# One call of a weight load moved ahead in a fused attention and GLU kernel: the first raw weights of f follow the first operands of q and M in the load queue

## The chip, the core and the metric

The kernel runs on one core of one Trainium2 chip. Its metric is the device time of one execution in microseconds (us), lower being better. Before the change it takes 731.56 us, the median of three runs (731.47 to 731.98).

## What is computed

All tensors are float32; S = 2048 tokens, D = 640, 32 heads of 20, F = 1536. The inputs are x, the weights wqkv, wo, w_gate, w_up, w_down, and a vector gate_w.

```python
qkv = (x @ wqkv).reshape(B, S, 3, H, Dh)            # q, k, v per head
phi = lambda t: where(t > 0, t + 1, exp(t)) + 1e-6
pq, pk = phi(q), phi(k)
kv  = einsum("bhsd,bhse->bhde", pk, v);  z = einsum("bhsd->bhd", pk)
num = einsum("bhqd,bhde->bhqe", pq, kv); den = einsum("bhqd,bhd->bhq", pq, z)
a = (num / (den + 1e-6)) @ wo                        # linear attention block
b = (sigmoid(x @ w_gate) * (x @ w_up)) @ w_down      # gated linear unit
g = sigmoid((x * gate_w).sum(-1))
out = g * a + (1 - g) * b
```

## The kernel before

**Numbers.** Every large float32 product is made of three matmuls: each operand is split into a high part (rounded to the matmul's format, written by ScalarE, ACT) and a low part (the rest, by a subtraction on VectorE, DVE), and TensorE (PE) adds high by high, low by high and high by low (helper `mm3`, lines 407 to 409; the split is lines 420 and 424). A split therefore is one ACT instruction and one DVE instruction, in that order.

**Stages.** The tokens are four groups of 512 columns, worked on in two pairs; pair 1 here is the first. The stages, in order of time, are: the k products and G = x^T phi(k); then, in `q_phase`, the q products of the first pair of groups, with the attention matrices M made beside them; then, in `f_phase`, the GLU of that pair; then q and GLU of the other pair with the weight forms read back from scratch memory; at the end the products with M and the output. The products of a pair use a seven-product scheme for two by two blocks: a unit n such as ("q", 1, 0) or ("f", 1, 0) goes through steps s1 to s7 (class `Block`), and needs three forms of its weights, wg (form 0), wu (form 1) and ws (form 2, sums of blocks, made in two parts).

**Weights of a unit.** `load_w` (line 1300) takes the next unit of the list `w_loads`, which is q(1,0), f(1,0), f(1,1) and so on, and issues one DMA of 640 KB from SyncE's queue (SP) into the next of the two buffers of the tile `wst`. The two buffers are used in turn. `queue_g` and `queue_s` then queue the work that makes the forms out of it: the split to wg, the split to wu, five sums on DVE that are made in place, and two splits to ws (`s_part`, line 1353: part 0 of 640 columns, part 1 of 512 columns). Behind the low part of part 1, the last reader of the buffer, `s_part` calls `load_w` (line 1362) for the next unit. Two more calls stand by themselves: line 1560, before M's first loads, for q(1,0), and line 2273 in `q_phase`, at step s6 of its unit A, for f(1,1).

**The order of work around the change.** In `q_phase` of pair 1 PE works through A = q(1,2), whose forms come ready from scratch memory, and B = q(1,0), whose forms are made from `wst`: A1, A2, two plain units, B1, B2, A3 to A7, B3 to B7. Between these stand the pieces of M for six groups of heads: `kv_part` (line 1624; a product on PE into PSUM tile `rot`, line 1629, then kvt, kvh, kvl on DVE) and `m_part` (line 1640; six matmuls of 320 columns with woh, wol, kvh, kvl into two PSUM tiles, each copied out to `ms`). The wo weights of a group come by a DMA into `wo_sb` (two buffers) and are split to woh and wol by `wo_split` (line 1612), which also issues the load of the group after next. `kv_part(5)` and `m_part(2)` stand between A5 and A6, `m_part(3)` between A7 and B3, `m_part(4)` and `m_part(5)` between B4, B5 and B6.

**Who orders it.** PE's order is written out by hand in the code. ACT's and DVE's is made while the program is built: a planner (class `Order`) keeps an estimated time of every engine and of every DMA, and each time that PE's work has been added, it adds those pieces of queued work whose data would have come and which would not delay PE (`fill`, line 116). A piece that is urgent (`first=True`: the split to wg of f(1,0), the wo splits) goes ahead of the others as soon as its data is there by that estimate; `order.need(key)` forces a piece out where PE needs it. On the chip each engine runs its list strictly in order, so an instruction that waits holds all behind it. SP's queue is also a list in order: an issue that waits for a buffer holds the issues behind it. GpSimd (POOL) has a queue of its own for the stores: each unit's forms go to scratch memory (wq, wf), each q result to p_dram, each piece of M to m_dram.

The queue of SP at this place: wst of q(1,0) (line 1560), three wv_sb, two wo_sb, then ws and wu of q(1,2) (lines 1662 and 1663), and from there only loads that other work calls for as buffers come free.

Of the kernel before, what the change touches and what calls it, by code (L numbers as in the profile page):

```python
# [367 lines left out]
def a_cost(w):  # L368
    return 0.06 + w / 1200

def v_cost(w):
    return 0.07 + w / 960

@with_exitstack
def gated_mix_kernel(ctx: ExitStack, tc: tile.TileContext, xt, xn, wk, wv, wo, wst_q, wst_f, out_t):
# [6 lines left out]
    order = Order()  # L382
# [3 lines left out]
    def f32(ap):  # L386
        return ap.bitcast(F32)
# [49 lines left out]
    def split(hi, lo, src, after=""):  # L437
        act(hi, src, AF.Copy, after)
        at = order.act + A_LAG

        def low():
            order.vec = max(order.vec, at)
            vec2(lo, src, f32(hi), OP.subtract)
        order.then(low)

    def add(out, a, b, after=""):
        vec2(out, a, b, OP.add, after)

    def sub(out, a, b, after=""):
        vec2(out, a, b, OP.subtract, after)  # L450
# [680 lines left out]
    for c in range(1, 4):  # L1131
# [37 lines left out]
        if c == 3:  # L1169
# [19 lines left out]
            def put(n, i, t):  # L1189
                WT[n, i] = t  # L1190
                W[n, i] = [t[:, c] for c in range(2)]

            def store_w(n, i):

                key = n[::2] + (i,)
                w_dram[key] = dram.tile(list(WT[n, i].shape), F32, name="w%s%d%d" % key)
                gp.dma_start(w_dram[key], f32(WT[n, i]))
# [81 lines left out]
    def wu_tile():  # L1279
        return pw.tile([P, 2, 3 * P], F32R, name="wu", tag="wu", bufs=2)  # L1280
# [3 lines left out]
    def ws_tile():  # L1284
        ws_n.append(0)
        return (pz if len(ws_n) % 2 == 0 else pw).tile([P, 2, 9 * P], F32R, name="ws", tag="ws")

    def load_form(n, i):
        t = (wg_tile, wu_tile, ws_tile)[i]()
        w = t.shape[2]  # L1290
        for c0, c1 in ((0, 2 * P), (7 * P, w), (5 * P, 7 * P), (2 * P, 5 * P)) if n == ("f", 0, 0) and i == 2 else ((0, w),):
            sp.dma_start(f32(t[:, :, c0:c1]), w_dram[n[::2] + (i,)][:, :, c0:c1])
        put(n, i, t)
# [6 lines left out]
    def load_w():  # L1300
        t = pw2.tile([P, 2, D], F32, name="wst", tag="wst", bufs=2)
        if not w_loads:
            t = t.rearrange("p k c -> p (k c)").rearrange("p (k c) -> p k c", c=CW)
            sp.dma_start(t, xt[len(c1_x), :, :, CW:])
            c1_x.append(t)
            other[-1].at = order.when(t)
            return
        n = w_loads.pop(0)
        sp.dma_start(t, wst_f[n[2], :, 0:2] if n[0] == "f" else wst_q[:, 0:2])
        WST[n] = t  # L1310
        W_AT[n] = t
# [10 lines left out]
    def w_due(n, s):  # L1322
        return {"stream": ("w", n), "due": order.due((*n[1:], s))} if n[0] == "f" and n[1:] + (1,) in order.plan else {}
# [6 lines left out]
    def queue_s(n, first=0, last=2):  # L1330

        def sums(part):
            g, u = WST[n][:, 0], WST[n][:, 1]
            c = [slice(2 * i * P, 2 * (i + 1) * P) for i in range(2)]
            if part == 0:
                order.need(("wg", n), False)
                order.need(("u", n), False)
                add(u[:, c[1]], u[:, c[0]], u[:, c[1]])
                sub(u[:, c[0]], g[:, c[0]], u[:, c[0]])
            else:  # L1340
                sub(g[:, c[0]], u[:, c[1]], g[:, c[0]])
                sub(g[:, c[1]], g[:, c[1]], g[:, c[0]])
                sub(g[:, 4 * P:], g[:, 4 * P:], u[:, 4 * P:])
            SUM_AT[n, 1 - part] = order.vec + V_LAG

        def u_part():
            put(n, 1, wu_tile())
            split(*W[n, 1], WST[n][:, 1, 2 * P:])
            order.then(lambda: store_w(n, 1))

        cut = (0, 5 * P, 9 * P)

        def s_part(part):
            if part == 0:
                put(n, 2, ws_tile())
            h, l = W[n, 2]
            cs = slice(cut[part], cut[part + 1])
            order.act = max(order.act, SUM_AT[n, part])
            split(h[:, cs], l[:, cs], WST[n][:, part, :cut[part + 1] - cut[part]])
            if part:  # L1360
                order.then(lambda: store_w(n, 2))
                order.then(load_w)

        if first == 0:
            order.add(a_cost(3 * P), v_cost(3 * P), u_part, ("u", n), lambda: order.when(W_AT[n]) if n in W_AT else 1e9, **w_due(n, 3))
            order.add(0, 2 * v_cost(2 * P), lambda: sums(0), **w_due(n, 3))
            order.add(0, 3 * v_cost(2 * P), lambda: sums(1), **w_due(n, 3))
        if last > 1:
            for part in range(2):
                w = cut[part + 1] - cut[part]  # L1370
                order.add(a_cost(w), v_cost(w), lambda part=part: s_part(part), ("w", n, part),
                          lambda part=part: SUM_AT.get((n, part), 1e9), **w_due(n, 3 + part))
# [288 lines left out]
    sp.t = max(sp.t, freed[1])  # L1661
    load_form(("q", 1, 2), 2)
    load_form(("q", 1, 2), 1)

    down_pool, down_cms = [], []
    HT, DST, WD, DS, DS_AT = {}, {}, {}, {}, {}
# [1395 lines left out]
```

## Time and profile before

| what | value |
|---|---|
| time, median of three runs | 731.56 us |
| the profiled execution, its own time | 731.82 us |
| span of the profile, first to last instruction | 730.1 us |
| TensorE busy (matmuls) | 719.4 us, 99% of the span |
| VectorE busy | 583.3 us, 80% |
| ScalarE busy | 371.0 us, 51% |
| GpSimd busy | 117.1 us, 16% |
| mean granted TensorE clock | 0.995 of full speed |
| DMA | 191.95 MB, mean 263 GB/s |

How to read it: the page gives one execution. Its time stands 1.7 us above its span, for what lies before the first and behind the last instruction, and 0.26 us above the median of the runs. A timeline row gives the start of an instruction, its length, engine, line and tiles (out<-in), and in brackets the idle time of the engine just before it with what ended that. Rows of PE overlap, since a matmul's end is modelled: a matmul of 512 columns has a length of 0.39 us, but the next starts 0.23 us after it. SPq and POOL rows of DMA are issues, not transfers.

### The profile page before, as it was taken

How to read it: one execution, taken by the hardware profiler on the slowest of the kernel's cores; microseconds unless marked ns; L12 is line 12 of the kernel's file. 1: busy time of each engine (PE TensorE's matmuls, PEld its weight loads, DVE VectorE, ACT ScalarE, POOL GpSimd, SP SyncE). 2: the span in 40 equal slices, each digit the busy share in tenths (PEclk: the TensorE clock that was granted, in tenths of full speed). 3: DMA queues.
4: the chain of work that ended last, by engine and by line, in shares of the span. 5: the costliest groups of instructions: out<-in, count | busy, mean ns of one | idle time of the engine just before them, and what ended most of it. 6: DMA issues, size and time to landing. Idle time of an engine off the chain costs nothing.

```text
span 730.1 us, 9886 instructions
## 1 busy us (share of the span) xinstructions
PE 719.4 (99%) x3395; PEld 607.4 (83%) x3395; DVE 583.3 (80%) x1009; ACT 371.0 (51%) x685; POOL 117.1 (16%) x189
## 2 busy tenths in 40 slices
PE   9999999996999999999999999999999999999998
PEld 8999898885888888888888888888888888888887
DVE  6888878784778889898989988357696968799895
ACT  6784647363755763535354855345424241544451
POOL 0211113132311221311211134001010111002300
PEclk9999999998999999999999999999999999999999
DMA  7677687967867866767787979978979895959957
GB/s 255 160 224 184 181 203 185 346 198 276 290 235 263 317 228 244 260 225 267 273 293 291 311 254 346 410 260 269 357 251 309 258 391 180 408 214 336 225 104 236
DMA packets 78889, 191.95 MB, mean 263 GB/s; under 512 B 8394, under 2 KB 37018, under 8 KB 75126
## 3 DMA queue, kind: packets, MB, share of 16 engines
q1 hardware_dynamic: 57654, 117.72, 48.9%
q0 software_dynamic: 20896, 73.36, 30.1%
q8 instruction: 27, 0.44, 0.2%
q10 hardware_dynamic: 288, 0.23, 0.1%
q14 instruction: 24, 0.20, 0.1%
HBM read 113.46 MB, written 75.52 MB: 259 GB/s over the span
## 4 chain that ended last, share of the span: by engine, by line
PE 93%; DMA 3%; DVE 2%; ACT 1%; SPq 0%; issue 0%; ACTq 0%; DVEq 0%
PE ch L407 11%; PE ch L408 11%; PE ch L409 11%; PE cc L407 9%; PE cc L408 9%; PE cc L409 9%; PE dd L407 6%; PE dd L408 6%; PE dd L409 6%; PE rot L407 5%; PE rot L409 5%; PE rot L408 5%; DMA ws<-wq 1%; DMA wst<-wst_f 1%; PE dd L2787 1%; DVE xtl L424 1%
## 5 line engine op out<-in xcount | busy, mean ns | idle before, releaser
L420 ACT ACTIVATE c<-ch 128x512 f32<-128x512 f32 x54 | 32.2, 596 | 81.2 <-PE ch L409 80.3
L424 DVE TENSOR_TENSOR hf<-c,hf 128x512 fp32r<-128x512 f32 x80 | 54.4, 686 | 19.3 <-ACT hf L420 18.9
L420 ACT ACTIVATE hf<-c 128x512 fp32r<-128x512 f32 x80 | 49.0, 625 | 31.1 <-DVE c L424 31.0
L424 DVE TENSOR_TENSOR c<-cc,c 128x512 f32<-128x512 f32 x42 | 28.9, 688 | 27.4 <-PE cc L409 17.9
L408 PE MATMUL ch<-xtl,ws 128*128 128x512 f32 x112 | 43.6, 389 | 0.0
L407 PE MATMUL ch<-xth,ws 128*128 128x512 f32 x112 | 43.6, 389 | 0.0
L409 PE MATMUL ch<-xth,ws 128*128 128x512 f32 x112 | 43.6, 389 | 0.0
L424 DVE TENSOR_TENSOR c<-c,c 128x512 f32<-128x512 f32 x52 | 35.7, 687 | 3.3 <-ACT c L420 2.7
L424 DVE TENSOR_TENSOR tb<-rot,tb 128x512 f32<-128x512 f32 x56 | 36.1, 682 | 0.3 <-PE rot L409 0.3
L407 PE MATMUL dd<-xrh,wg 128*128 128x512 f32 x90 | 35.1, 390 | 0.0
L408 PE MATMUL dd<-xrl,wg 128*128 128x512 f32 x90 | 35.0, 389 | 0.0
L409 PE MATMUL dd<-xrh,wg 128*128 128x512 f32 x90 | 35.0, 389 | 0.0
L420 ACT ACTIVATE c<-dd 128x512 f32<-128x512 f32 x22 | 13.1, 596 | 41.4 <-PE dd L409 41.3
L407 PE MATMUL cc<-xbh,ws 128*128 128x512 f32 x84 | 32.9, 392 | 0.0
L408 PE MATMUL cc<-xbl,ws 128*128 128x512 f32 x84 | 32.9, 392 | 0.0
L409 PE MATMUL cc<-xbh,ws 128*128 128x512 f32 x84 | 32.9, 392 | 0.0
L424 DVE TENSOR_TENSOR tb<-dd,tb 128x512 f32<-128x512 f32 x36 | 24.7, 686 | 9.3 <-PE dd L409 9.2
L420 ACT ACTIVATE dd<-ch 128x512 f32<-128x512 f32 x22 | 12.8, 582 | 35.9 <-PE ch L409 35.9
L407 PE MATMUL ch<-xth,wu 128*128 128x512 f32 x56 | 22.5, 402 | 6.1 <-ACT c L420 6.1
L424 DVE TENSOR_TENSOR tb<-cc,tb 128x512 f32<-128x512 f32 x36 | 24.5, 684 | 1.9 <-PE cc L409 1.9
L424 DVE TENSOR_TENSOR wst<-wst 128x256 f32<-128x256 f32 (+1 forms) x65 | 24.6, 395 | 1.4
L409 PEld LDWEIGHTS ch<-xth,ws 128*128 128x128 f32 x112 | 21.0, 188 | 4.7 <-DVE ws L424 0.2
(690 smaller groups left out, 2329.2 us busy)
## 6 DMA issues: line engine op xcount, KB each, us to landing
wf<-ws POOLq DMA_DIRECT2D x12, 1152.0 KB, 7.5
ws<-wf SPq DMA_DIRECT2D x11, 1152.0 KB, 8.1
wst<-wst_f SPq DMA_DIRECT2D x12, 640.0 KB, 4.9
wf<-wg POOLq DMA_DIRECT2D x12, 640.0 KB, 6.5
wd<-wd POOLq DMA_DIRECT2D x12, 640.0 KB, 7.7
wg<-wf SPq DMA_DIRECT2D x12, 640.0 KB, 5.3
wf<-wd SPq DMA_DIRECT2D x10, 640.0 KB, 11.6
xnst<-xn SPq DMA_DIRECT2D x16, 320.0 KB, 4.0
```

The source lines that it names most:

```text
L407: nc.tensor.matmul(out, l_hi, r_hi, start=first, stop=False, skip_group_check=True)
L408: nc.tensor.matmul(out, l_hi, r_lo, start=False, stop=False, skip_group_check=True)
L409: nc.tensor.matmul(out, l_lo, r_hi, start=False, stop=last, skip_group_check=True)
L420: nc.scalar.activation(out, src, fn, **kw)
L424: nc.vector.tensor_tensor(out, a, b, op=op)
L2787: nc.tensor.matmul(ps, l, r, start=new, stop=j == 1 and k == ks[-1], skip_group_check=True)
```

## The change

The call of `load_w` behind the last split of a unit's raw weights is made only for units of f. A call for f(1,0) is added right behind the two loads of q(1,2)'s forms ws and wu, at the head of the stage. The list of loads is the same, with the same two buffers, and so is the call at step s6 of A for f(1,1).

```diff
             split(h[:, cs], l[:, cs], WST[n][:, part, :cut[part + 1] - cut[part]])
             if part:
                 order.then(lambda: store_w(n, 2))
-                order.then(load_w)
+                if n[0] == "f":
+                    order.then(load_w)
...
     load_form(("q", 1, 2), 2)
     load_form(("q", 1, 2), 1)
+    load_w()
```

On SP's queue, at the head of the q stage, the order shows one load in another place; wst<-wst_f is the load of an f unit's raw weights, ws<-wq and wu<-wq are the forms of q(1,2).

```order
 L364 DMA ws<-wq_470 128x2304
 L364 DMA wu<-wq_469 128x768
+L364 DMA wst<-wst_f 128x1280
 L364 DMA wo_sb<-wo 100x640
 L364 DMA wv_sb<-wv 128x500 x2
 L364 DMA wo_sb<-wo 100x640
 L364 DMA wv_sb<-wv 128x500
-L364 DMA wo_sb<-wo 100x640
-L364 DMA wst<-wst_f 128x1280
-L364 DMA wo_sb<-wo 100x640
+L364 DMA wo_sb<-wo 100x640 x2
 L364 DMA wst<-wst_f 128x1280 x2
```

The load of f(1,0) has moved ahead of six loads of M's operands; the loads of wo for groups 4 and 5 now stand together.

On ACT, between steps A3 and A6, the planner places the splits otherwise; c_1624 and c_1803 are results of q, dd and ms belong to `m_part`, wg<-wst is the split of f(1,0), ws<-wst the last split of q(1,0). Before:

```order
L420 ACTIVATE c_1624<-c_1624 128x512
L420 ACTIVATE ms<-dd_1816 120x320
L420 ACTIVATE ms<-dd_1821 120x320
L420 ACTIVATE woh<-wo_sb 100x640
L420 ACTIVATE ws<-wst 128x512
L420 ACTIVATE woh<-wo_sb 100x640
L420 ACTIVATE wg<-wst 128x640
L420 ACTIVATE c_1883<-ch_1616 128x512
L420 ACTIVATE ms<-dd_1896 100x320
L420 ACTIVATE ms<-dd_1901 100x320
L420 ACTIVATE woh<-wo_sb 100x640
L420 ACTIVATE qe<-c_1883 128x512
```

And after the change (c_1626 is the tile that was c_1624):

```order
L420 ACTIVATE c_1626<-c_1626 128x512
L420 ACTIVATE wg<-wst 128x640
L420 ACTIVATE ms<-dd_1818 120x320
L420 ACTIVATE ms<-dd_1825 120x320
L420 ACTIVATE woh<-wo_sb 100x640 x2
L420 ACTIVATE ws<-wst 128x512
L420 ACTIVATE c_1883<-ch_1618 128x512
L420 ACTIVATE ms<-dd_1896 100x320
L420 ACTIVATE ms<-dd_1901 100x320
L420 ACTIVATE qe<-c_1883 128x512
L420 ACTIVATE c_1883<-c_1883 128x512
L420 ACTIVATE woh<-wo_sb 100x640
```

The split to wg of f(1,0) no longer stands right ahead of c_1883<-ch, the copy that empties the PSUM tile of A5, but five instructions further up; the split to woh of group 4 stands two rows later.

On DVE at the same place the low parts follow; kvt, kvh, kvl belong to `kv_part` of groups 3 and 4, the first wol<-wo_sb to group 2. Before:

```order
L428 SCALAR_TENSOR_TENSOR qe<-qe,c_1624 128x512
L424 TENSOR_TENSOR kvt<-rot_1827,bd 100x100
L868 CAST kvh<-kvt 100x100
L424 TENSOR_TENSOR kvl<-kvt,kvh 100x100
L424 TENSOR_TENSOR wol<-wo_sb,woh 100x640
L424 TENSOR_TENSOR kvt<-rot_1841,bd 100x100
```

And after:

```order
L428 SCALAR_TENSOR_TENSOR qe<-qe,c_1626 128x512
L424 TENSOR_TENSOR wg<-wst,wg 128x640
L424 TENSOR_TENSOR kvt<-rot_1831,bd 100x100
L868 CAST kvh<-kvt 100x100
L424 TENSOR_TENSOR kvl<-kvt,kvh 100x100
L424 TENSOR_TENSOR kvt<-rot_1848,bd 100x100
L868 CAST kvh<-kvt 100x100
L424 TENSOR_TENSOR kvl<-kvt,kvh 100x100
L424 TENSOR_TENSOR wol<-wo_sb,woh 100x640 x2
```

The low part of group 2's wo now stands behind wg and behind the kv pieces of both groups 3 and 4. PE's own list is the same before and after. Three smaller moves go with it: on POOL the store of f(1,0)'s wg stands ahead of that of q(1,0)'s ws; and in the first step of `f_phase` the split to wg of f(1,1) stands three rows earlier on ACT (ahead of the load of the sigmoid's table) and two earlier on DVE, with its store one place earlier on POOL.

## Prediction

> **What bounds the kernel now.** First the page: the span, and TensorE's granted clock in 40 slices of 18.25 us.
>
> ```profile
> span 730.1 us, 9886 instructions
> ...
> PEclk9999999998999999999999999999999999999999
> ```
>
> PE is busy for 99% of the span, so its own work is the bound; one slice, the tenth (164 to 182 us), has a lower clock. The waits of PE and then the chain of waits between 155 and 180 us say what happens there.
>
> ```profile
> PE ch L407 <- ACT c L420: 6.1, 1, 6.1
> ```
>
> ```profile
> 164.44 7.22 DMA wst<-wst_f
> ```
>
> One wait of 6.1 us is nearly all that PE loses to other engines. It ends on ACT's copy of a PSUM tile, but the chain runs through that copy back to a load: wst<-wst_f, the raw weights of f(1,0), issued at 164.44 and landed 7.22 us later. The timelines show why a load for a later stage stops PE. SP, the loads:
>
> ```profile
> 135.19 0.42 SPq L364 DMA_DIRECT2D wu<-wq  x1
> 145.60 0.31 SPq L364 DMA_DIRECT2D wo_sb<-wo  x1
> ...
> 164.08 0.30 SPq L364 DMA_DIRECT2D wo_sb<-wo  x1
> ```
>
> ACT, ahead of the stop and at it:
>
> ```profile
> 161.24 0.63 ACT L420 ACTIVATE c<-c 128x512 f32<-128x512 f32 x1
> 161.78 0.75 ACT L420 ACTIVATE ms<-dd 120x320 f32<-120x320 f32 x2
> 162.41 0.74 ACT L420 ACTIVATE woh<-wo_sb 100x640 fp32r<-100x640 f32 x1
> ...
> 171.68 0.74 ACT L420 ACTIVATE wg<-wst 128x640 fp32r<-128x640 f32 x1 [7.37 <-DMA wst<-wst_f]
> 172.32 0.58 ACT L420 ACTIVATE c<-ch 128x512 f32<-128x512 f32 x1
> ```
>
> And PE at the same place:
>
> ```profile
> 164.92 0.31 PE L407 MATMUL dd<-woh,kvh 100*100 100x320 f32 x1
> 165.06 0.30 PE L408 MATMUL dd<-wol,kvh 100*100 100x320 f32 x1
> ...
> 172.95 0.79 PE L407 MATMUL ch<-xth,wu 128*128 128x512 f32 x1 [6.11 <-ACT c L420]
> ```
>
> ACT comes to the split to wg at 164.3 us and sits there for 7.37 us. Right behind it in ACT's list stands c<-ch, which empties the PSUM tile that A5 filled; A6, at 172.95, writes that tile again. A5's matmuls had all started before 164.92, so the copy itself was ready when ACT stopped, within a microsecond.
>
> **The change part by part: what it removes.** The load leaves SP some 29 us sooner, behind wu at 135.19. Even at the 7.22 us of the old load it lands near 143, and at twice that before 151; ACT now comes to wg when it ends c<-c, at 161.87. So the 6.1 us go. A little more goes with them, because that idle time counts from a modelled end: PE's rows overlap by some 0.2 us (164.92 plus 0.31, against the next start at 165.06). I put the hole at 6.3 us. Nothing else is late in its place: the copy then waits only for A5 and ends before 166, and A6 has a `m_part` and a `kv_part` of PE ahead of it until about 166.6.
>
> The hole has a tail. By windows, with the granted clock in the third column from the end: the hole's middle, its end, A6 with A7, and B6 with B7, which are the same eighteen matmuls.
>
> ```profile
> 167.00:171.00 4.00, 0.00 (x0) 0.00 (x0) 0.00 (x0) 0.00 (x0) 0.00 (x0) 1.00 1.02 376
> 171.00:172.95 1.95, 0.00 (x0) 0.00 (x1) 0.51 (x1) 1.27 (x3) 0.00 (x0) 0.61 0.58 244
> 172.95:179.64 6.69, 6.69 (x19) 5.24 (x19) 4.33 (x9) 3.98 (x8) 1.98 (x4) 0.60 0.76 242
> 187.10:191.27 4.17, 4.17 (x21) 3.46 (x19) 2.53 (x5) 2.88 (x6) 1.76 (x4) 1.00 0.77 218
> ```
>
> The clock falls while PE idles and is low for most of A6 and A7: 6.69 us against 4.17. Without the hole it does not fall, so 6.69 - 4.17 = 2.5 us go too. Together 8.8 us.
>
> The Trainium skill, "TensorE: Matmul & The Clock Gate", section "What's actually happening", states that about 3.4 us without work halve the clock and about 3.4 us of work restore it. By that the tail would be half of 3.4, an estimate of 1.7 us, and the time 0.8 us above the one forecast here. The trace agrees on the cause, but its rows show a longer tail, and the measurement decides.
>
> **What it moves.** On DVE, wg and both kv pieces now stand ahead of the wol of group 2, which PE's second matmul of `m_part(2)` reads (the one at 165.06). Before, one kv piece did.
>
> ```profile
> 162.52 0.25 DVE L424 TENSOR_TENSOR kvt<-rot,bd 100x100 f32<-100x100 f32 x1
> ...
> 163.23 0.82 DVE L424 TENSOR_TENSOR wol<-wo_sb,woh 100x640 fp32r<-100x640 f32 x1
> ...
> 172.44 0.83 DVE L424 TENSOR_TENSOR wg<-wst,wg 128x640 fp32r<-128x640 f32 x1 [7.07 <-ACT wg L420]
> 173.19 0.82 DVE L424 TENSOR_TENSOR wol<-wo_sb,woh 100x640 fp32r<-100x640 f32 x1
> ```
>
> wg takes 0.75 us of DVE (172.44 to 173.19), a kv piece 0.71 (162.52 to 163.23). So wol starts at 163.23 + 0.75 + 0.71 = 164.69 and ends, with its 0.82, at 165.51. Its woh is ready: on ACT wg takes 0.64 (171.68 to 172.32), woh moves from 162.41 to 163.05 and ends by 163.8. PE wants wol at 165.06 and waits 0.45, call it 0.5 us: a new stall. Its bounds are nothing, if pieces fit into gaps, and 1.5 us, the whole of the 1.46 put ahead.
>
> In f's first step, the split of f(1,1) now stands ahead of the sigmoid and of the copy behind it, first ACT, then PE:
>
> ```profile
> 196.23 0.60 ACT L420 ACTIVATE c<-ch 128x512 f32<-128x512 f32 x1
> ```
>
> ```profile
> 198.07 0.39 PE L407 MATMUL ch<-xth,ws 128*128 128x512 f32 x1
> ```
>
> The copy ended at 196.83, 1.24 us before PE wanted its tile. Put ahead of it are ACT's wg, 0.64, and, through the sum that the sigmoid reads, DVE's wg, 0.75: 1.39 in all. So 0 to 0.15 us; I take 0.1. The two swaps on POOL are stores to scratch memory that only the other pair's stage reads back; they cost nothing while the DMAs keep up.
>
> The issue itself costs SP 0.4 us, as wu's, where its next issue is at 145.60, ten us later. The load brings 640 KB, 1.7 us at the 376 GB/s of the window 167 to 171, in among the transfers of 136 to 147 us. What is most exposed to it is the chain gt_dram, back, gt; the instructions on the tile back, and its landing times:
>
> ```profile
> L364 POOL DMA_DIRECT2D back<-gt_dram x4: 558/560/581, 145.5 to 147.1; - x4
> L420 ACT ACTIVATE gt<-back x1: 727/727/727, 159.5 to 159.5; 128x640 f32<-128x640 f32 x1
> ...
> DMA to landing us min/median/max: 4.6/5.6/6.0
> ```
>
> The last issue at 147.1 lands by 153.1 with the longest of these, and ACT reads back at 159.5: 6.4 us of cover for 1.7. The wo_sb issued at 145.60 has until 162.41. So the load costs nothing where it goes.
>
> **The sum.** 6.3 + 2.5 - 0.5 - 0.1 = 8.2 us. The profiled execution took 731.82, 1.7 above its span; it would take 723.6, and the median, 0.26 lower, 723.4. All behind this place only moves earlier, since PE waits for nothing there. I add 0.1 for losses that the next rival brings close: 723.5. The forecast's own bounds are 722.7 (no new stall at all: 731.56 - 8.8) and 724.6 (wol's full 1.5 us and 0.15 in f).
>
> **The rivals.** First, a shorter wait takes the old one's place, on ACT at the split of group 4's wo. Its load goes out when group 2's wol has been read: at 164.08 before, right behind 163.23 + 0.82; now at about 165.5. On ACT that split stands ahead of A6's copies, of f(1,0)'s splits and of B5's copy, for which B6 waits. That copy had 0.2 us to spare before, and loads of wv and wo had these landing times (the last column):
>
> ```profile
> 186.41 0.60 ACT L420 ACTIVATE c<-ch 128x512 f32<-128x512 f32 x1 [0.20 <-PE ch L409]
> ```
>
> ```profile
> wv_sb<-wv SPq DMA_DIRECT2D x4, 250.0 KB, 5.1
> ...
> wo_sb<-wo SPq DMA_DIRECT2D x2, 300.0 KB, 7.0
> ```
>
> The copy is due at 186.41 - 8.3 = 178.1. From the split to it ACT has three rows of 640 columns (0.64 each, as 171.68 to 172.32), nine of up to 512 (0.54, as 161.24 to 161.78) and a pair of ms (0.63, as 161.78 to 162.41), an estimate of 7.4 us. So the split must start by 170.7, 5.2 us behind the issue. The row of 5.1 just holds, the row of 7.0 is 1.8 us too long: 725.3. For the forecast: the stretch was full at 376 GB/s with the 640 KB in it, which are now gone from there. For the rival: the store of f(1,0)'s wg now goes ahead. Chance 0.11.
>
> Second, only the wait goes and the clock still falls near here, from several small stalls or by itself: 723.5 + 2.5 = 726.0. Against it, the clock is 1.00 up to 171 us, with 4 us of idleness in that, and falls only then. Chance 0.05.
>
> Third, the change does not do what it says: ACT's copy was held by something that ended together with the load, and the wait stays: 731.6. Against it, nothing stands between wg and the copy in ACT's list, and DVE's 7.07 us end on the same split. Chance 0.03.
>
> Fourth, slower: the early load holds up the transfers beside it. "DMA: Bandwidth & Descriptors" of the Trainium skill, section "Issuing engines are not separate DMA queues", states that transfers run on the same 16 engines and interleave, whichever engine issued them. The mechanism here is ACT's gt<-back: if back lands late, ACT's list stops, and with it A3's copy and PE. It begins to cost at 6.4 us of delay, one for one, and makes the kernel slower from 6.4 + 8.1 = 14.5; at 16 us the time is 723.5 + 9.6 = 733.1. For it, the two wo loads issued shortly ahead took 7.0 us for 300 KB (the row above), so transfers crowd here already; against it, 1.7 us of added transfer would have to grow ninefold. No run shows such a delay. Chance 0.03.
>
> **How the numbers follow.** The forecast has 0.78, the rivals 0.11, 0.05, 0.03 and 0.03. A difference under 0.2% (1.5 us) could not be told from none here. The forecast and the first two rivals are faster by more than that: 0.94; the third is the same, 0.03; the fourth slower, 0.03. The range runs from the forecast's lower bound, 722.7, to the second rival, 726.0. The predicted time is the forecast's, 723.5.
>
> **What would show it.** In the profile after, the 6.1 us wait is gone from PE's waits, the tenth slice has a full clock, and A6 with A7 take 4.2 us. The load is issued near 136, and ACT's wg runs at 162 with no idle time ahead. A wait of PE of 0.5 us on DVE's wol near 165 would confirm the new stall. ACT idle at the woh of group 4, and PE at B6, would be the first rival; a half clock without a hole the second; the old 7.4 us at something else the third; idle time ahead of gt<-back the fourth. The prediction is wrong if PE's time from 164.92 to the end of A7, 14.7 us before, does not fall to about 6.4, or if as much is lost again behind it.

## The result and the profile after

The changed kernel takes 726.55 us, the median of four runs (726.34 to 727.22), against 731.51 for the kernel before in runs beside it: a ratio of 0.9932, 95% interval 0.9915 to 0.9949. Measured again (run e5 below) it takes 726.29, ratio 0.9923 (0.9909 to 0.9936). So it is faster by about 5 us, and 3 us slower than forecast: outside the range. The profiled execution took 726.68 us.

The hole is gone, and its tail with it. The page, PE's waits, and the window of A6 and A7:

```profile
span 725.0 us, 9883 instructions
...
PEclk9999999999999999999999999999999999999999
```

```profile
PE dd L407 <- DVE c L424: 0.6, 1, 0.6
PE cc L407 <- DVE c L424: 0.5, 1, 0.5
PE dd L408 <- DVE wol L424: 0.5, 1, 0.5
PE dd L407 <- DVE ms L868: 0.3, 1, 0.3
```

```profile
168.19:172.36 4.17, 4.17 (x21) 3.45 (x20) 1.69 (x5) 1.57 (x3) 1.60 (x3) 1.00 0.92 249
```

The wait of 6.1 us no longer stands among PE's waits, the tenth slice has a full clock, and A6 with A7 take 4.17 us and not 6.69. Four small waits are listed instead; the first, 0.6 us on DVE's c, lies at 160.05, ahead of the hole's place, and was 0.3 us before the change. PE's list is the same in both kernels, so the start of each matmul can be compared one by one; where the distance between the two traces jumps, PE gained or lost time, and below this is called the loss "by the starts":

| place in the trace after | change, us | forecast |
|---|---|---|
| hole and half clock, to the end of A7 | -8.83 | -8.8 |
| `m_part(2)`, 166.6, on wol | +0.69 | +0.5 |
| `m_part(5)` and B7, 179.4 and 183.1, on DVE's ms and c | +1.22 | 0 |
| first step of f, 188.8 (0.33) and 192.6 (0.39) | +0.73 | +0.1 |
| first 7 us of the kernel (0.61), and 160.0 (0.30) | +0.90 | 0 |
| everywhere else | +0.14 | 0 |
| sum | -5.15 | -8.2 |

Two engines show how the third row comes about. SP and ACT after the change:

```profile
138.20 0.33 SPq L364 DMA_DIRECT2D wst<-wst_f  x1
...
166.54 1.21 SPq L364 DMA_DIRECT2D wo_sb<-wo  x2
```

```profile
162.69 0.72 ACT L420 ACTIVATE wg<-wst 128x640 fp32r<-128x640 f32 x1
...
169.15 0.63 ACT L420 ACTIVATE c<-c 128x512 f32<-128x512 f32 x1
172.05 0.74 ACT L420 ACTIVATE woh<-wo_sb 100x640 fp32r<-100x640 f32 x1 [2.28 <-DMA wo_sb<-wo]
```

The early load is issued at 138.2 (near 136 was forecast), and wg is split at 162.69 with no idle time. But the loads of wo for groups 4 and 5 wait for a buffer until 166.54, and ACT comes to group 4's split 3.2 us later and idles for 2.28 us. Before, ACT came to it 9.4 us after the issue (164.08), because it had stood in the hole. The row of before:

```profile
173.43 0.75 ACT L420 ACTIVATE woh<-wo_sb 100x640 fp32r<-100x640 f32 x1
```

DVE and PE behind it, after the change:

```profile
172.82 0.83 DVE L424 TENSOR_TENSOR wol<-wo_sb,woh 100x640 fp32r<-100x640 f32 x1 [2.32 <-ACT woh L420]
...
175.01 0.55 DVE L424 TENSOR_TENSOR wu<-wst,wu 128x384 fp32r<-128x384 f32 x1
...
178.85 0.88 DVE L868 COPY ms<-dd 100x320 f32<-100x320 f32 x2
...
182.32 0.68 DVE L424 TENSOR_TENSOR c<-cc,c 128x512 f32<-128x512 f32 x1
```

```profile
179.39 0.39 PE L407 MATMUL dd<-woh,kvh 100*100 100x320 f32 x1 [0.27 <-DVE ms L868]
...
183.06 0.50 PE L407 MATMUL cc<-xbh,ws 128*128 128x512 f32 x1 [0.47 <-DVE c L424]
```

From wu on DVE has no gap down to c, and PE waits for two of its results. In the first step of f the chain of waits runs back to a store:

```profile
181.36 5.51 DMA p_dram<-qe
...
186.95 0.64 ACT qe L420
...
188.73 0.63 ACT wg L420
...
190.82 0.61 DVE c L424
...
191.45 1.13 ACT c L420 x2
...
192.62 0.50 PE ch L407
```

The group of tiles that qe belongs to has four buffers, and the new qe at 186.95 takes the one whose store to p_dram went out at 181.36 and landed 5.5 us later. The split of f(1,1), wg at 188.73, stands in the same chain. So two things delay PE in this step, the store and that split; e2 and e7 below tell them apart.

### The profile page after: what moved, and what is told of

Same layout as the page of the kernel before. It is cut to its first block, busy times and chain, and to the rows that moved or that the text cites. A ratio compares the mean times of both kernels' runs of the same rounds, so it can differ in the third digit from the quotient of the medians.

```text
span 725.0 us, 9883 instructions
## 1 busy us (share of the span) xinstructions
PE 718.9 (99%) x3395; PEld 606.2 (84%) x3395; DVE 583.1 (80%) x1009; ACT 371.1 (51%) x685; POOL 116.8 (16%) x189
## 4 chain that ended last, share of the span: by engine, by line
PE 91%; DMA 3%; issue 2%; DVE 2%; POOL 1%; ACT 1%; POOLq 0%; ACTq 0%; DVEq 0%
PE ch L407 10%; PE ch L408 10%; PE ch L409 10%; PE cc L407 8%; PE cc L408 8%; PE cc L409 8%; PE dd L407 6%; PE dd L408 6%; PE dd L409 6%; PE rot L407 5%; PE rot L409 5%; PE rot L408 5%; DMA wst<-wst_f 2%; DMA wst<-wst_q 1%; DMA p_dram<-qe 1%
## 5 line engine op out<-in xcount | busy, mean ns | idle before, releaser
L407 PEld LDWEIGHTS ch<-xth,ws 128*128 128x128 f32 x112 | 21.0, 188 | 5.0 <-ACT c L420 0.9
L409 PEld LDWEIGHTS ch<-xth,ws 128*128 128x128 f32 x112 | 21.0, 188 | 4.7 <-DVE ws L424 0.3
## 6 DMA issues: line engine op xcount, KB each, us to landing
wf<-wd SPq DMA_DIRECT2D x10, 640.0 KB, 10.4
```

Source lines behind the costliest of these rows:

```text
L407: nc.tensor.matmul(out, l_hi, r_hi, start=first, stop=False, skip_group_check=True)
L409: nc.tensor.matmul(out, l_lo, r_hi, start=False, stop=last, skip_group_check=True)
```

## The experiments

Fourteen runs are named e1 to e14. Thirteen have a time; e3, the changed kernel with a fifth buffer for the tiles that qe belongs to, has none, because a later pool of 40 KB per partition then has only 38 KB left. A diff is against the changed kernel where nothing else is said.

### Is it the order, or the load? (e1, e4)

The first theory put all small waits down to the new order of the splits. In e1 the split to wg of f(1,0) is queued one step later, and every list of ACT, DVE and PE is that of the kernel before, with the early load:

```diff
-                    elif blk is A and s == 3:
+                    elif blk is A and s == 4:
                         queue_g(("f", pr, 0))
```

> The early load, with ACT's and DVE's instructions in the order of the kernel before (the split to wg of f(1,0) is queued one step later, so that it stands right ahead of A5's copy again, and f(1,1)'s split behind the sigmoid). Theory: the 3 us by which the change fell short are small stalls of the new order, so they go: no wait of PE on wol near 166, group 4's wo is issued near 165 and not at 166.5, ACT idles less than 1 us ahead of that woh or reaches it 1.5 us sooner than at 172.05, and no wait of PE on c or ms near 179 and 183. Time 723.9 us (723.2 to 724.8), 2.6 below the changed kernel's 726.55. Rival, the early load itself costs (640 KB among the transfers of 136 to 147 us, and what it brings forward): the time stays near 726.5.

726.64 us (726.18 to 726.90). The theory fell. The wait on wol is gone, as expected, and others are there. ACT in e1, and PE's waits there:

```profile
169.26 0.74 ACT L420 ACTIVATE woh<-wo_sb 100x640 fp32r<-100x640 f32 x1 [2.26 <-DMA wo_sb<-wo]
...
176.45 0.74 ACT L420 ACTIVATE woh<-wo_sb 100x640 fp32r<-100x640 f32 x1 [3.23 <-DMA wo_sb<-wo]
```

```profile
177.73 0.50 PE L407 MATMUL ch<-xth,ws 128*128 128x512 f32 x1 [1.02 <-ACT c L420]
...
180.04 0.39 PE L407 MATMUL dd<-woh,kvh 100*100 100x320 f32 x1 [0.66 <-DVE ms L868]
...
181.73 0.50 PE L407 MATMUL ch<-xth,wu 128*128 128x512 f32 x1 [0.57 <-ACT c L420]
```

Group 4's load goes out sooner (164.65), ACT comes to it sooner too, and idles as long as before; then it idles 3.23 us more at group 5's. The time is the rival's, but not for its reason: from 136 to 165 us PE waits only 0.5 us, on DVE's c, a wait that the kernel before has too.

e4 is the other half: the kernel before, its load late as ever, and only the split queued later (diff against the kernel before):

```diff
-                    elif blk is A and s == 3:
-                        queue_g(("f", pr, 0))
...
                     elif blk is A and s == 7:
+                        queue_g(("f", pr, 0))
                         queue_s(("f", pr, 0))
```

> The kernel before with its late load, in which only the split to wg of f(1,0) is queued later, behind A6's results and ahead of the split to wu. Theory: the hole came from the place of the wait in ACT's list and not from the time of the load as such; the load lands near 171.7, ACT comes to wg near 171, and PE's 6.1 us and the clock's fall go without an earlier load: 723.2 us (722.7 to 724.5). Rival: the load, issued at 164.4, is too late for whatever place; ACT idles over 3 us at wg and PE waits behind it, and the time stays over 726.

726.99 us (726.03 to 729.41, six runs), ratio 0.994 (0.9924 to 0.9957): as much as the change brings, without its load. ACT, and the chain of waits at the same place:

```profile
169.19 0.74 ACT L420 ACTIVATE woh<-wo_sb 100x640 fp32r<-100x640 f32 x1 [2.65 <-DMA wo_sb<-wo]
...
171.97 0.74 ACT L420 ACTIVATE wg<-wst 128x640 fp32r<-128x640 f32 x1
...
176.02 0.74 ACT L420 ACTIVATE woh<-wo_sb 100x640 fp32r<-100x640 f32 x1 [2.25 <-DMA wo_sb<-wo]
```

```profile
166.27 9.73 DMA wo_sb<-wo
```

The hole came from the place of the wait in ACT's list, as its theory said; f(1,0)'s load, issued at 164.57, is there for wg at 171.97 with no idle time. The number was 3.8 us off, and not for the rival's reason: ACT again waits for wo, group 5's load taking 9.73 us. Early load or late, old order or new, the time is 726.3 to 727.0 us. So what is left is likely common to all, and the two late loads of wo are; the next runs test them.

### The wo loads (e6, e9, e10, e11)

In e6 wo_sb has three buffers:

```diff
-            o = mp.tile([bdn, D], F32, name="wo_sb", tag="wo_sb", bufs=2)
+            o = mp.tile([bdn, D], F32, name="wo_sb", tag="wo_sb", bufs=3)
...
-        order.then(lambda: load_mo(hg + 2))
+        order.then(lambda: load_mo(hg + 3))
...
     load_mo(1)
+    load_mo(2)
```

> The changed kernel with three buffers for wo_sb, so that the loads of groups 4 and 5 no longer wait for the splits of groups 2 and 3 (group 4's goes out near 150 us and not at 166.5, group 5's near 164). Theory: with the hole gone the next limit is when these two loads go out; ACT's 2.3 us ahead of woh of group 4 go, and with them PE's waits on ms and c at 179 and 183, 1.2 us; the loss in the first step of f stays: 725.3 us (724.6 to 726.0). Rival: the DMAs have too much to move between 165 and 190, whatever the buffers; the loads or stores behind come later by as much, and the time stays at 726.5.

724.62 us (724.28 to 725.50), 1.7 below the changed kernel on the same chip. ACT, and all of PE's waits on other engines:

```profile
167.97 0.73 ACT L420 ACTIVATE woh<-wo_sb 100x640 fp32r<-100x640 f32 x1
...
173.88 0.73 ACT L420 ACTIVATE woh<-wo_sb 100x640 fp32r<-100x640 f32 x1
```

```profile
PE dd L408 <- DVE wol L424: 0.5, 1, 0.5
PE dd L407 <- DVE c L424: 0.4, 1, 0.4
```

The theory holds for the waits on ms and c at 179 and 183: both are gone with ACT's idle time (the wait on c that is left is the one near 160). Its number was too high by 0.7, since the loss in the first step of f, which was to stay, went as well. But the planner, seeing other times, had also put f(1,1)'s split back behind the sigmoid. e9 forces that one ahead again; beside the buffer only group 4's woh, two rows up on ACT, and its wol on DVE then stand elsewhere (diff against e6):

```diff
                     queue_g(("f", pr, 1))
+                    order.need(("wg", ("f", pr, 1)), False)
```

> The changed kernel with the third wo_sb buffer and with f(1,1)'s split where the changed kernel has it (in e6 the planner had also put that one back), so that the buffer, and group 4's woh two rows earlier on ACT, are all that differ. Theory: the late loads of wo are the cause also of the loss in the first step of f, because they delay the stores to p_dram; f1's split costs 0.15 us at most: 724.7 us (724.2 to 725.2), like e6. Rival: f(1,1)'s split costs more by itself; the first step of f loses over 0.4 us again and the time is over 725.2.

725.13 us (724.27 to 725.80): 1.2 below the 726.29 of e5, with no loss at `m_part(5)` and B7 by the starts, and with 0.6 us of loss in the first step of f. The time is just inside the theory's range, the loss is the rival's. But the profile has the wait for the store again, ahead of that split in ACT's list, so the split isn't alone in it:

```profile
184.75 0.63 ACT L420 ACTIVATE qe<-c 128x512 f32<-128x512 f32 x1 [1.78 <-DMA p_dram<-qe]
```

e10 puts e6's edit on the kernel before. The planner then moves the split to wg of f(1,0) behind A6's results by itself.

> The kernel before, with its late load, and the third wo_sb buffer; the planner then puts the split to wg of f(1,0) behind A6's results by itself, as in the run with the order alone. Theory: once no wait stands ahead of A5's copy and the wo loads are out early, the place of f(1,0)'s load does not matter: 723.9 us (723.3 to 724.8). Rival: a load issued at 164.4 lands too late for the split at 169.5 as well, ACT idles there for 2 us or more, and the time is over 725.5.

724.65 us (723.40 to 725.94), ratio 0.99 (0.9886 to 0.9915): with the load late, more by the medians than the change brought. Within its theory's range; ACT idles 1.24 us at wg, not 2, and 2.62 at the store of qe, behind which PE loses 1.5 us by the starts.

```profile
171.51 0.74 ACT L420 ACTIVATE wg<-wst 128x640 fp32r<-128x640 f32 x1 [1.24 <-DMA wst<-wst_f]
...
186.12 0.63 ACT L420 ACTIVATE qe<-c 128x512 f32<-128x512 f32 x1 [2.62 <-DMA p_dram<-qe]
```

e11 is e1 with e6's edit.

> The early load with the order of the kernel before (as in the run with the load alone) and the third wo_sb buffer. Theory: without the waits of 2.3 and 3.2 us of ACT at the splits of groups 4 and 5, and with wol of group 2 in its old place, PE waits for nothing from 160 to 200 us: 723.7 us (723.2 to 724.3), level with the run of all three edits, though f(1,2)'s load is where it was. Rival: f(1,2)'s load beside the store to p_dram still costs 0.5 us or more: 724.3 or over.

724.27 us (722.87 to 725.43), at the border between the two. The trace speaks for the rival: by the starts PE loses 0.5 us in the first step of f, where ACT idles 2.13 us at qe. The profile puts that wait down to DVE, but the store to p_dram landed 0.08 us before it ended, as in e5 (0.09 in e2). Against e1, 726.64, the third buffer is worth 2.4 us there, and by the starts the three losses of e1 from 177 to 182 us, 2.9 us together, are gone.

### The first step of f (e2, e7)

e2 puts f(1,1)'s split back where the kernel before has it, and nothing else:

```diff
-                if s == 1 and not f:
+                if s == 2 and not f:
                     queue_g(("f", pr, 1))
-                elif s == 2 and not f:
                     queue_s(("f", pr, 1))
```

> The changed kernel with only f(1,1)'s split to wg put back behind the sigmoid, as before the change. Theory: that split, 0.64 us of ACT and 0.75 of DVE, is what makes PE lose 0.7 us in the first step of f (at 189 and 192.6 us), so the time is 725.8 us. Rival: the loss there comes from ACT's 1.6 us at qe, which waits for a store to p_dram to land; then the time stays at 726.5 and that wait stays in the profile.

725.75 us (724.91 to 726.21): the number its theory gave, but the profile has the reason only in part. ACT and PE in e2:

```profile
186.39 0.63 ACT L420 ACTIVATE qe<-c 128x512 f32<-128x512 f32 x1 [2.47 <-DMA p_dram<-qe]
```

```profile
188.22 0.50 PE L407 MATMUL ch<-xth,ws 128*128 128x512 f32 x1 [0.80 <-ACT c L420]
```

With the split out of the way ACT waits longer for the store, and PE loses 1.1 us in that step in this trace, more than the 0.73 after the change. What this execution had ahead of the changed kernel's, it had ahead of 160 us, so the time decides nothing here. By the starts the step holds two losses, and both theories have a part. The first, at the matmul of 188.22 (188.8 after the change), is the store's: 1.09 us here. The second, at 192.6 after the change, goes with the split: it is 0.35 to 0.44 us in all five traces that have f(1,1)'s split ahead of the sigmoid (after, e5, e7, e9, e14), and nothing in e2 and the eight others that have it behind.

e7 takes away what runs beside that store: the load of f(1,2)'s raw weights, 640 KB, which goes out behind the last split of f(1,0), and is not read before f's second step.

```diff
-                if n[0] == "f":
+                if n[0] == "f" and n[2]:
                     order.then(load_w)
...
                 if s == 1 and not f:
+                    load_w()
                     queue_g(("f", pr, 1))
```

> The changed kernel with the load of f(1,2)'s raw weights issued in f's first step and no longer behind the last split of f(1,0)'s, near 182 us. Theory: those 640 KB run beside the store of qe to p_dram and make it land late; without them ACT's wait of 1.6 us (2.5 in the run with f(1,1)'s split late) for that store, and PE's 0.7 to 0.8 us behind it, go: 725.7 us (725.2 to 726.3). Rival: the store lands late for its own sake or for the store of f(1,0)'s ws beside it; the wait and the time stay.

725.50 us (725.29 to 727.57), 0.8 below e5, and no wait for the store; ACT waits for DVE at that place, as it did before the change:

```profile
186.66 0.63 ACT L420 ACTIVATE qe<-c 128x512 f32<-128x512 f32 x1 [1.36 <-DVE c L424]
```

The intervals of e5 and e7 overlap (0.9909 to 0.9936 and 0.9909 to 0.9934), so the time alone does not carry it. The traces say more. The lists of PE, ACT, DVE and POOL are those of the changed kernel, and the store lands in 2.7 us, where it took 5.5 (after) and 6.6 (e5); the first loss in f's step, 0.33 and 1.30 there, is 0.02. The second stays, 0.43 us, and ACT's wait that leads to it is there without any late store:

```profile
191.16 0.63 ACT L420 ACTIVATE c<-c 128x512 f32<-128x512 f32 x1 [0.80 <-DVE c L424]
```

Over all traces without the hole, that store takes 5.5 to 6.7 us in six of the ten that have f(1,2)'s load in its old place, and 2.7 to 4.2 us in the four (e7, e8, e12, e13) that have it in f's first step. But in e1, e4, e6 and e14 the load goes out 1.07 us behind the store, as after the change, and the store lands in 2.4 to 4.3 us all the same. So the load is part of the cause and not all of it; what else it takes stays open.

### The same kernel again (e5)

> The changed kernel once more, beside the next three on one chip: to see how far its executions differ and where. Theory: PE's waits of 0.4 to 0.8 us in the stretch from 176 to 196 us (on ms, c, and in the first step of f) come back in the same places, and the time is 726.5 us (726.0 to 727.0). Rival: the half microsecond that the profiled execution lost in its first 6 us, and 0.3 near 159, are part of the change; then they come back too.

726.29 us (725.81 to 727.57; the profiled execution is the slowest). PE's waits come back at B7 (0.5) and in the first step of f, where one is 1.0 us; at `m_part(5)` none is listed, but by the starts PE loses 0.37 us there. The losses behind 170 us belong to the change, then, but not each in its size. The 0.3 near 160 us does not come back and is no part of it: that wait, on DVE's c, is 0.3 us before the change, and anything from none to 0.8 in the other runs. Half a microsecond in the first 7 us does come back (0.47), but in e2, with the same beginning, it is absent (0.16 us ahead of the kernel before), and in e10, with the load late, it is 0.62; it is told of at the end.

### All edits together, and one taken out (e8, e12, e13)

e8 has e6's third buffer, e7's late load of f(1,2), and e4's place for the split to wg of f(1,0). With these, the planner has also put f(1,1)'s split back behind the sigmoid, where the kernel before has it; so it stands in e12 and e13.

> Three edits on the changed kernel: the third buffer for wo_sb, f(1,2)'s load in f's first step, and the split to wg of f(1,0) queued behind A6's results, so that DVE's wol of group 2 stands where it stood before the change. Theory: nothing of PE's waits between 160 and 200 us is left but 0.3: 723.5 us (723.0 to 724.4), as the prediction had it. Rival: a further wait takes their place, and the time is over 725.

723.71 us (723.58 to 723.75), ratio 0.9889 (0.9876 to 0.9903). All that PE still waits for is its own sequencer, at its first matmul; the waits on ms, c and wol are gone:

```profile
PE rot L502 <- PEq L3056: 0.8, 1, 0.8
```

This is the time that the prediction gave for the change. It beats both kernels, by 8.0 and 2.6 us.

e13 is e8 with the split to wg where the changed kernel has it; e12 is e8 with f(1,0)'s load late: ACT's, DVE's, POOL's and PE's lists are the same as e8's, and only that one load stands elsewhere on SP.

> The changed kernel with the third wo_sb buffer and f(1,2)'s load in f's first step, but with the split to wg of f(1,0) where the changed kernel has it, ahead of wol of group 2 on DVE. Theory: PE's wait on that wol, 0.5 us, is all that it has over the run with all three edits: 724.2 us (723.8 to 724.8), and the profile shows no wait of PE over 0.3 us from 170 to 200 us. Rival: the wait on wol is made up for behind it, and the time is 723.7.

> The kernel before with the third wo_sb buffer and f(1,2)'s load in f's first step. Every engine's list is that of the run with all three edits; only f(1,0)'s load is back behind the last split of q(1,0), near 164.7 us. Theory: the early load is worth little once nothing urgent stands behind its split; it lands near 171.5, ACT idles about 1.2 us at the split to wg as in the run before, and PE loses 0.3 us at B7: 724.0 us (723.6 to 724.7). Rival: the early load itself is worth more, because ACT's and DVE's lists have no room there; the time is 725 or over.

e13: 723.97 us (723.80 to 724.55), inside its theory's range and 0.26 above e8; the profile has the wait on wol, 0.44 us (0.69 by the starts), and no other from 160 to 200 us. e12: 724.76 us (724.26 to 724.91), just above its theory's range and 1.05 above e8, whose interval (0.9876 to 0.9903) overlaps with e12's (0.9881 to 0.9922). ACT and PE in e12:

```profile
171.87 0.74 ACT L420 ACTIVATE wg<-wst 128x640 fp32r<-128x640 f32 x1 [1.49 <-DMA wst<-wst_f]
```

```profile
181.44 0.50 PE L407 MATMUL cc<-xbh,ws 128*128 128x512 f32 x1 [0.28 <-DVE c L424]
```

The load issued late still comes 1.49 us late for ACT, and by the starts, against e8, 0.75 us of it reaches PE: 0.27 ahead of B7 and 0.48 at B7. So the edit under study is itself worth some 0.75 us (the profile) to 1.05 us (the medians, whose intervals overlap) where nothing else is in the way.

### Why a load of 250 KB takes 5.5 us (e14)

```diff
-            sp.dma_start(o[:w], wo[c0:c0 + w])
+            if w % 16:
+                m = w // 16 * 16
+                sp.dma_start(o[:m], wo[c0:c0 + m])
+                sp.dma_start(o[m:w], wo[c0 + m:c0 + w])
+            else:
+                sp.dma_start(o[:w], wo[c0:c0 + w])
```

> The changed kernel with each load of wo cut into two, 96 rows and 4 rows (112 and 8 for the first two groups); all lists of PE, ACT, DVE and POOL are the same. It asks why group 4's load takes 5.5 us for 250 KB, when loads of 640 KB have a median of 5.3. The Trainium skill, DMA: Bandwidth & Descriptors, section on why a DMA increments its semaphore by 16, states that a transfer runs on the largest number of engines up to 16 that divides its rows, 10 for 100 rows and 16 for 96. Theory, the row count makes it slow: ACT's wait of 2.2 to 2.4 us ahead of that woh falls below 1.0 and the time to 725.6 us (725.0 to 726.0). Rival, the transfers beside it make it slow: the wait stays over 1.7 us and the time at 726.4.

727.75 us (726.47 to 729.20), by the medians slower than the changed kernel, though the intervals overlap (0.9926 to 0.9961 against 0.9909 to 0.9936 in e5). ACT at groups 4 and 5:

```profile
171.20 0.74 ACT L420 ACTIVATE woh<-wo_sb 100x640 fp32r<-100x640 f32 x1 [1.56 <-DMA wo_sb<-wo]
...
177.21 0.74 ACT L420 ACTIVATE woh<-wo_sb 100x640 fp32r<-100x640 f32 x1 [3.24 <-DMA wo_sb<-wo]
```

Group 4's load, issued at 166.40, lands in 4.8 us instead of 5.5, and group 5's, behind it, now makes ACT idle for 3.24 us where it made it idle for none. Neither theory holds: 96 rows gain 0.7 us at one load, and the other loses more. Nor is the gain sure: in e1 group 4's load, uncut, was there 4.6 us behind its issue (164.65 to 169.26). The question itself compared unlike things: 5.3 us is the median of the twelve loads of wst over the whole kernel, and the one issued in this stretch, at 167.88 after the change, took 10.4 us. How many DMA engines a load of 100 rows runs on, no run here shows; why loads are slow in this stretch stays open.

## Why the prediction was wrong

**What held.** The removed wait and its tail: 8.8 us forecast, 8.83 measured, with the mechanism as told (the load, ACT's split, the copy behind it, the clock). By the section of the Trainium skill that the prediction names for it ("TensorE: Matmul & The Clock Gate", "What's actually happening") the tail would have been 0.8 us shorter and the two together 8.0; the trace bears out the longer tail. The new wait on group 2's wol: 0.5 forecast, 0.45 in PE's row, 0.69 by the starts; e8 against e13 shows that it goes when wg is split later. PE's time from the first matmul of `m_part(2)` to the end of A7 fell from 14.7 to 6.6 us.

**The step that failed** is the sentence "All behind this place only moves earlier, since PE waits for nothing there". PE waited for nothing there because ACT, DVE and the loads had had the hole to catch up in; without it, 1.22 us were lost at `m_part(5)` and B7 and 0.73 in f's first step. Of the 2.6 us between the medians of e5 and e8, the runs give 1.2 to the two buffers of wo_sb (e9 against e5; by the starts the loss at `m_part(5)` and B7 is gone in e9), about 0.8 to f(1,2)'s load beside the store (e7 against e5, not clear of noise), 0.3 to wol, which had been counted (e13 against e8), and by the starts 0.4 to f(1,1)'s split. That is 2.7 us; the small ones are no larger than the scatter of the medians.

**The first rival had the mechanism** and was given 0.11. Its price was worked out along one path alone. The deadline for group 4's split, 170.7 us, came from ACT's own list, the copy for B6 with 0.2 us to spare. DVE's list was not followed. There stood, in the trace of before, a run without a gap from wu to the c that B7 reads:

```profile
180.45 0.55 DVE L424 TENSOR_TENSOR wu<-wst,wu 128x384 fp32r<-128x384 f32 x1
...
188.10 0.69 DVE L424 TENSOR_TENSOR c<-cc,c 128x512 f32<-128x512 f32 x1
```

It ends at 188.79, and B7 begins at 189.23: 0.44 us to spare. PE's work behind A7 comes 7.25 us sooner after the change, so wu was due at 180.45 - 7.25 + 0.44 = 173.6. It started at 175.01, 1.4 us late, and PE lost 1.22. On ACT's path alone nothing was lost: B6 did not wait. The landing time was the lesser fault: 5.5 us, against 5.2 allowed and the row of 5.1 that was taken for it.

**The term for f's first step**, 0.1 us, was too small twice over. It counted f(1,1)'s split at its busy time, 1.39 us against 1.24 to spare, and so at most 0.15; the split cost 0.35 to 0.44 us. The busy time leaves out that DVE also idles for ACT's part of the split, 1.15 us after the change and 0.87 in e7. And it put the transfers at nothing "while the DMAs keep up". They did not, though not shown to be by the two swaps of stores: in e2 the second is undone, and the wait for the store stays. A window of 5 us, before and then after, has each engine's busy time first and at the end the clock, the share of DMA time and GB/s:

```profile
170.00:175.00 5.00, 2.05 (x5) 1.67 (x6) 2.56 (x4) 2.86 (x6) 1.09 (x2) 0.64 0.51 215
```

```profile
170.00:175.00 5.00, 5.00 (x26) 4.27 (x25) 2.53 (x4) 2.95 (x7) 0.77 (x2) 1.00 0.98 351
```

The two windows hold the same stretch of time and not the same work: before, it is the hole's end. From 165 to 195 us the DMA share after the change is 0.80 to 1.00 in every such window; before, it fell to 0.51 here and lay at 0.60 to 0.70 from 180 to 190. The same loads and stores now have 8.8 us less to go in.

**What was not foreseen and is not the change's.** The 0.90 us up to 160 us come, as far as the runs show, from the two executions that were compared. The first 0.61 lie ahead of 7 us, where the lists of all engines are the same; the 0.30 lie at a place where the other traces, early load or late, have anything from 0.4 us less to 0.55 us more than the trace of before.

## What to carry to other kernels

A long wait of the bounding engine is also the time in which everyone else catches up. Before its whole length is counted as a gain, go through each load and store issued in it and shortly behind it, and hold its issue-to-landing time against the new, earlier time of its reader, along every engine's list and not only the one that held the wait. And ask of a late load that stops an engine whether the load is late or its reader stands too far ahead: here moving the reader alone did as much as moving the load.

## What the runs showed of the hardware

The first 7 us of one and the same list of matmuls took from 0.23 us less (e12, e13) to 0.86 us more (e6) than in the trace of before. Pairs of matmuls of 322 columns, before and after the change:

```profile
5.66 0.45 PE L1065 MATMUL ch<-k1h,xal 128*128 128x322 f32 x2
5.95 0.45 PE L1065 MATMUL dd<-k3l,xah 128*128 128x322 f32 x2
```

```profile
6.00 0.70 PE L1065 MATMUL ch<-k1h,xal 128*128 128x322 f32 x2
6.54 0.47 PE L1065 MATMUL dd<-k3l,xah 128*128 128x322 f32 x2
```

They start 0.29 us apart in the one and 0.54 in the other until 6.54. The Trainium skill, "TensorE: Matmul & The Clock Gate", "Part 1: The HAM clock gate", states that the clock's window runs freely, so that the number of cold matmuls, those at the low clock, at a kernel's start varies from run to run. The trace agrees: its record of the granted clock begins, at full clock, at 4.17 us before the change and at 6.53 after, 4.70 in e2 and 6.85 in e6. The difference to the trace of before is 0.61 us after the change, 0.86 in e6, and -0.16 in e2. That is as much as some of these edits bring, so single traces should be compared behind it.

Loads of 250 KB took from 4.6 us (e1) to 9.73 us (e4) to land while the DMAs were 0.9 to 1.0 busy, and a load of 640 KB took 10.4 us among them, where the twelve loads of wst have a median of 5.3 us over the kernel.
